# A gated linear-attention recurrence with a mixture of experts on one core: which chunks have their triangular blocks inverted together

## The chip, the cores and the metric

The kernel runs on one core of a Trainium2 chip, as one launch. The metric is the device time of that launch in microseconds (us). The engines are TensorE (PE in the profile; PEld is its weight load), VectorE (DVE), ScalarE (ACT), GpSimd (POOL) and SyncE (SP), which in this kernel only issues DMAs. Each engine runs its instructions in the order in which the program lists them, and waits on semaphores for what the others produce.

## The reference, cut to what matters

For 4 batches and 8 heads there are 768 steps of a 40 x 40 state per head. Each step reads the state, decays it, corrects it by a rank-one term and adds a rank-one term; the attention output then goes through 8 experts:

```python
for t in range(S):                                  # S = 768
    y[:, :, t] = np.einsum('bhd,bhde->bhe', rt, state)
    Sa = np.einsum('bhde,bhe->bhd', state, at)
    state_decay = state * wt[:, :, None, :] - np.einsum('bhd,bhe->bhde', Sa, bt)
    state = state_decay + np.einsum('bhd,bhe->bhde', vt, kt)
...
P = np.exp(x @ w_gate - max)                        # x: 3072 tokens x 320
for _ in range(8):                                  # rows and columns of P normed in turn
    ...
for e in range(E):                                  # E = 8, F = 1024
    out += P[:, e:e + 1] * (np.maximum(x @ w1[e], 0.0) @ w2[e])
```

## The kernel before, in words

**Chunks.** The 768 steps are cut into 12 chunks of 64 steps (c = 0 to 11). Within a chunk the rank-one corrections couple the steps by a strictly triangular 64 x 64 matrix per head, so that a chunk can be done with matmuls once the inverse of the unit triangular matrix is there. Work on a chunk is done per batch, b = 0 to 3, all 8 heads at once. Below, "chunk 9 b0" is batch 0 of chunk 9.

**Preparation** (`prep`, lines 106 to 165), once for each chunk and batch, does not need the state: a load of the inputs (`inp`, line 109), scans on DVE (lines 114 to 124: `q`, a reciprocal, `g`), products on POOL (`cc`, `ab`, `kb`; for the first ones on DVE), matmuls `ll` and transposes `kt` on PE, a mask on DVE (line 155), copies on ACT. The triangular blocks go out of `lt` to DRAM (`ld`, line 148 or 164). Its results are kept in 17 sets of buffers (NSX = 17), used in rotation. So a preparation can run ahead of the recurrence by 17 batches, a little over four chunks, and then waits for a set: preparation number 4c + b writes the set that number 4c + b - 17 has used.

**Inversion.** Line 388 lists groups of chunks that are inverted together. For each group the triangular 32 x 32 diagonal blocks are loaded back from DRAM with one block to a partition: `lu`, line 342, four DMAs for each chunk, which fills 64 partitions. So a pair of chunks takes all 128 partitions. The inversion itself is on DVE alone (lines 167 to 194): per group seven products and seven reductions on the small diagonal blocks (lines 170 and 173), then eight products (line 179) and eight reductions (line 182) on larger ones, then one copy (line 331) that puts the result in another order into the buffer `pr`. These are 31 instructions for any group; the number of chunks in it sets only how many partitions they cover (`us`, line 367). `un`, `lu` and `pr` have one buffer each. After the copy the inverses go to DRAM (`ud` and `nd`, lines 333 and 334) and come back in the layout of the recurrence (`tload`, lines 207 to 217: `lg`, `td`, `tt`). `tmat` (lines 219 to 233) joins the 32 x 32 blocks to 64 x 64 on PE (`gp`, `op`) and ACT.

**Recurrence** (`recur`, lines 235 to 302), for each chunk and batch, depends on the same batch of the chunk before: `av` on PE, the mask `f` on DVE (line 252), `xc` on PE, copies on ACT, `pu` on PE with the inverse `tt` (line 270), the mask `pm` on DVE (line 272), `c2` on PE, `ws` on DVE (line 279), the output `y` and the next state `z` (POOL; `z` on DVE from chunk 9 on), a transpose `zt` and copies into `vz`. The first instruction of a batch that needs the chunk's inverse is `pu`; `pm`, right behind it, is used below as the mark for where a chunk stands. The four batches of a chunk follow each other a few us apart.

**Order.** The events of preparation, inversion and recurrence are sorted by due times (lines 346 to 382). Inside the attention part a scheduler then places the instructions on each engine by its own estimate of their times; it decides which of them lie between the operations of an inversion. The mixture of experts (lines 449 to 734) comes behind: its weights and tokens are split and loaded (`prep_w`, `prep_x`) while the last chunks run, and from its ninth block on its order is written out by hand.

Of the kernel before, what the change touches and what calls it, by code (L numbers as in the profile page):

```python
# [28 lines left out]
def attention(ctx, tc, d, xd, ps, pq, pt, gs, lg):  # L29
# [328 lines left out]
    for c in range(NCH):  # L358
# [5 lines left out]
        for half in range(2):  # L364
            ev.append((t + 2 * SKEW * half, tmat, (c, half)))
    for s, cs in enumerate(GROUPS):
        us = slice(0, 64 * len(cs))
# [17 lines left out]
            pass  # L385


GROUPS = [[0, 1], [2, 3], [4, 5], [6, 7], [8, 9], [10, 11]]
GRP = {c: (i, j) for i, g in enumerate(GROUPS) for j, c in enumerate(g)}
P0 = -8  # L390
PD = 0.75
# [416 lines left out]
```

## Time and profile before

| | before |
|---|---|
| median of 3 runs | 1899.47 us (1899.22 to 1904.73) |
| span of the profiled execution, first to last instruction | 1898.1 us |
| PE busy | 1763.3 us (93%) |
| DVE busy | 1414.6 us (75%) |
| ACT busy | 863.0 us (45%) |
| POOL busy | 939.8 us (50%) |
| first `pm` of chunk 0, of chunk 11 | 125.70 us, 538.93 us from the start |
| start of the copy that ends an inversion (line 331), six of them | 103.43, 166.28, 264.33, 346.15, 428.13, 487.59 us |

The profile gives the profiled execution no time but its span; the median of the runs is 1.4 us above it. Times in the views are us from the start of that span. A row of the timeline has the start, the duration, the engine with its line and operation, and in brackets how long the engine sat idle before it and what ended that. "Busy" counts an instruction's whole duration, and the ends of matmuls are modelled, so that a busy PE need not be at its limit. A name such as `st` or `sx` on DVE's line 155 is one of the 17 sets.

### The profile page before, as it was taken

How to read it: one execution, taken by the hardware profiler on the slowest of the kernel's cores; microseconds unless marked ns; L12 is line 12 of the kernel's file. 1: busy time of each engine (PE TensorE's matmuls, PEld its weight loads, DVE VectorE, ACT ScalarE, POOL GpSimd, SP SyncE). 2: the span in 40 equal slices, each digit the busy share in tenths (PEclk: the TensorE clock that was granted, in tenths of full speed). 3: DMA queues.
4: the chain of work that ended last, by engine and by line, in shares of the span. 5: the costliest groups of instructions: out<-in, count | busy, mean ns of one | idle time of the engine just before them, and what ended most of it. 6: DMA issues, size and time to landing. Idle time of an engine off the chain costs nothing.

```text
span 1898.1 us, 31892 instructions
## 1 busy us (share of the span) xinstructions
PE 1763.3 (93%) x12035; PEld 1723.4 (91%) x12035; DVE 1414.6 (75%) x2330; ACT 863.0 (45%) x1861; POOL 939.8 (50%) x881
## 2 busy tenths in 40 slices
PE   4378989889898999999999999989999999999999
PEld 4368888788888999999999999989999999999999
DVE  7767778687588877676877768996776768777676
ACT  5336565655563444343343434444343433434342
POOL 5636355562254346282643718353562826437170
PEclk9569788989899999999999999999999999999999
DMA  8477776865631111020111102220110201111011
GB/s 189 95 131 149 149 148 136 162 133 123 158 112 62 37 37 55 19 73 19 55 37 37 57 17 73 77 82 34 40 55 19 73 19 55 37 37 55 19 37 42
DMA packets 188414, 139.67 MB, mean 74 GB/s; under 512 B 156005, under 2 KB 165349, under 8 KB 188261
## 3 DMA queue, kind: packets, MB, share of 16 engines
q1 hardware_dynamic: 185061, 132.39, 28.0%
q10 hardware_dynamic: 3200, 5.25, 1.1%
q8 instruction: 95, 1.56, 0.3%
q14 instruction: 58, 0.48, 0.1%
HBM read 117.15 MB, written 20.45 MB: 72 GB/s over the span
## 4 chain that ended last, share of the span: by engine, by line
PE 70%; DVE 10%; DMA 3%; issue 3%; POOL 1%; ACT 1%; SPq 0%; DVEq 0%; POOLq 0%; ACTq 0%
PE op L609 33%; PE p L544 31%; DVE hl L568 1%; PE xc L259 1%; DMA inp<-in_inp_dram 1%; DVE sm L562 1%; DVE pr L179 1%; PE pu L270 1%; PE av L251 1%; PE lp L307 1%; DVE xch L532 1%; PE ll L145 1%; DVE u L562 1%; DMA nd<-pr 1%; PE c L277 1%
## 5 line engine op out<-in xcount | busy, mean ns | idle before, releaser
L544 PE MATMUL p<-xch,wh 128*128 128x384 f32 (+1 forms) x1792 | 606.0, 340 | 13.1 <-DVE u L562 7.5
L565 ACT ACTIVATE hh<-sm 128x384 fp32r<-128x384 f32 x512 | 269.4, 526 | 730.0 <-DVE sm L562 730.0
L609 PE MATMUL op<-wh,hh 128*128 128x320 f32 x1536 | 477.1, 311 | 1.0 <-ACT hh L565 0.9
L609 PE MATMUL op<-wl,hh 128*128 128x320 f32 x1536 | 474.9, 310 | 0.0
L609 PE MATMUL op<-wh,hl 128*128 128x320 f32 x1536 | 468.1, 310 | 5.2 <-DVE hl L568 5.2
L490 POOL TENSOR_TENSOR wl<-ws,wh 128x640 fp32r<-128x640 f32 x64 | 110.7, 1730 | 573.0 <-ACT wh L488 572.8
L568 DVE SCALAR_TENSOR_TENSOR hl<-sm,hh 128x384 fp32r<-128x384 f32 x512 | 375.8, 767 | 2.8 <-ACT hh L565 2.3
L544 PEld LDWEIGHTS p<-xch,wh 128*128 128x128 f32 (+1 forms) x1792 | 337.6, 189 | 18.9 <-DVE u L562 10.3
L544 PE MATMUL p<-xcl,wh 128*128 128x384 f32 x896 | 302.8, 338 | 0.0
L544 PE MATMUL p<-xch,wl 128*128 128x384 f32 x896 | 302.4, 337 | 0.0
L609 PEld LDWEIGHTS op<-wh,hl 128*128 128x128 f32 x1536 | 287.0, 188 | 6.3 <-DVE hl L568 6.1
L609 PEld LDWEIGHTS op<-wh,hh 128*128 128x128 f32 x1536 | 290.5, 189 | 1.6 <-ACT hh L565 1.5
L609 PEld LDWEIGHTS op<-wl,hh 128*128 128x128 f32 x1536 | 291.2, 190 | 0.0
L562 DVE TENSOR_TENSOR sm<-p,u 128x384 f32<-128x384 f32 x384 | 236.4, 625 | 8.8
L544 PEld LDWEIGHTS p<-xcl,wh 128*128 128x128 f32 x896 | 168.8, 188 | 0.0
L544 PEld LDWEIGHTS p<-xch,wl 128*128 128x128 f32 x896 | 168.7, 188 | 0.0
L562 DVE TENSOR_TENSOR sm<-p,p 128x384 f32<-128x384 f32 x128 | 71.3, 557 | 127.8 <-PE p L544 72.6
L562 DVE TENSOR_TENSOR p<-p,p 128x384 f32<-128x384 f32 x128 | 71.1, 556 | 98.9 <-PE p L544 97.3
L562 DVE TENSOR_TENSOR u<-p,p 128x384 f32<-128x384 f32 x128 | 70.8, 553 | 56.6 <-PE p L544 55.4
L145 PE MATMUL ll<-ab,kb 104*128 104x128 f32 x336 | 61.7, 342 | 55.1 <-POOL ab L140 24.2
L498 POOL TENSOR_TENSOR wl<-ss,wh 128x512 fp32r<-128x512 f32 x64 | 96.8, 1513 | 32.1 <-ACT wh L495 27.6
L145 PEld LDWEIGHTS ll<-ab,kb 104*128 104x128 f32 x336 | 53.5, 242 | 59.3 <-POOL ab L140 30.1
(161 smaller groups left out, 2884.1 us busy)
## 6 DMA issues: line engine op xcount, KB each, us to landing
ws<-in_wts_dram SPq DMA_DIRECT2D x64, 832.0 KB
inp<-in_inp_dram SPq DMA_DIRECT2D x42, 521.6 KB
rb<-in_r_dram SPq DMA_DIRECT2D x48, 208.0 KB
ld<-lt ACTq DMA_DIRECT2D x40, 128.0 KB
vz<-in_v_dram SPq DMA_DIRECT2D x48, 104.0 KB
f<-in_vt_dram SPq DMA_DIRECT2D x48, 80.0 KB
xd<-y SPq DMA_DIRECT2D x96, 40.0 KB
st<-in_inp_dram SPq DMA_DIRECT2D x6, 521.6 KB
```

What stands on the lines that cost most here:

```text
L145: nc.tensor.matmul(ll[:, p], lhsT=kb[:, p], rhs=ab[:, p], start=True, stop=True)
L179: nc.vector.tensor_tensor(out=prv, in0=a.unsqueeze(2).broadcast_to([nu, n_c, n_r, n_k]), in1=m.rearrange("u k r -> u r k").unsqueeze(1).br ...
L251: nc.tensor.matmul(av[:, p], lhsT=vz[:, p], rhs=rb[:, p], start=True, stop=True)
L259: nc.tensor.matmul(xc[h][:, p], lhsT=pp["sx"][:, p, h], rhs=f[:, p, h], start=True, stop=True)
L270: nc.tensor.matmul(pu[:, p], lhsT=tts[c][:, b * NP + p], rhs=x1[:, p], start=True, stop=True)
L490: g.tensor_tensor(out=wl[:, 0:640], in0=raw[:, 256:896], in1=wh[:, 0:640], op=ALU.subtract)
L498: g.tensor_tensor(out=lv[:, 3:7], in0=so[:, :, 0], in1=hv[:, 3:7, 0], op=ALU.subtract)
L544: nc.tensor.matmul(o, lhsT=w_, rhs=x_, start=(j == 0), stop=(j == 3))
L562: eng.tensor_tensor(out=out, in0=x, in1=y, op=ALU.add)
L565: nc.scalar.activation(out=hh[:, f, h], in_=sm[f][:, h], func=AF.Relu)
L568: v.scalar_tensor_tensor(out=hl[:, f, h], in0=sm[f][:, h], scalar=0.0, in1=hh[:, f, h], op0=ALU.max, op1=ALU.subtract)
L609: nc.tensor.matmul(ops[i], lhsT=a[:, h, cs], rhs=w_[:, cw], start=(f == 0 and h == 0 and j == 0), stop=(last and h == 1 and j == 2))
```

## The change

Seven groups take the place of six. Chunk 0 is inverted alone, then come the pairs (1, 2), (3, 4), (5, 6), (7, 8) and (9, 10), and chunk 11 is inverted alone:

```diff
-GROUPS = [[0, 1], [2, 3], [4, 5], [6, 7], [8, 9], [10, 11]]
+GROUPS = [[0], [1, 2], [3, 4], [5, 6], [7, 8], [9, 10], [11]]
 GRP = {c: (i, j) for i, g in enumerate(GROUPS) for j, c in enumerate(g)}
```

The due times of the groups follow from the list (line 368: five units to a chunk, less ten), and so does the number of inversions. Nothing else is edited, but the scheduler's order comes out different on every engine.

On SP, at the start of the program, the loads of the first group's triangular blocks (line 342) stood so before, behind the last stores of `ld`:

```order
L148 DMA ld<-st_188 64x512
L342 DMA lu<-ld 16x32x32 x3
L148 DMA ld<-st_187 64x512
L342 DMA lu<-ld 16x32x32
L208 DMA lg<-ld 32x16x32 x2
L164 DMA ld<-lt 64x512 x2
L109 DMA inp<-in_inp_dram 104x1284
L342 DMA lu<-ld 16x32x32 x4
```

and stand so now:

```order
L148 DMA ld<-st_188 64x512
L342 DMA lu<-ld 16x32x32 x4
L148 DMA ld<-st_187 64x512
L208 DMA lg<-ld 32x16x32 x2
L164 DMA ld<-lt 64x512 x2
```

The first group needs four loads where it needed eight, and the second four, behind two stores of chunk 1's blocks and an input, are no longer in front of its first instruction.

On DVE, at the place where chunk 1's first `pm` (line 272) stood before, the second inversion, of chunks 2 and 3, was near its end (`sx_157` is the set of chunk 4 b3):

```order
L182 TENSOR_REDUCE un<-pr 128x16x8
L279 TENSOR_TENSOR ws<-c_1257,c_203 104x416
L114 SCALAR_TENSOR_TENSOR q<-inp,cst 104x260
L272 TENSOR_TENSOR pm<-pu,cst 128x416
L179 TENSOR_TENSOR pr<-gt,un 128x2048
L118 RECIPROCAL g_196<-q 104x4
L155 TENSOR_TENSOR sx_157<-ll,cst 64x8x64
L182 TENSOR_REDUCE un<-pr 128x16x8
```

The same `pm` now (the `L272` in the last row) stands behind the first operations of the third inversion, of chunks 3 and 4 (`sx_161` is the set of chunk 5 b0):

```order
L155 TENSOR_TENSOR sx_161<-ll,cst 64x8x64
L170 TENSOR_TENSOR pr<-un,lu 128x4
L312 COPY lg<-lp 64x8
L173 TENSOR_REDUCE un<-pr 128x4
L170 TENSOR_TENSOR pr<-un,lu 128x16
L173 TENSOR_REDUCE un<-pr 128x4x2
L170 TENSOR_TENSOR pr<-un,lu 128x36
L173 TENSOR_REDUCE un<-pr 128x4x3
L170 TENSOR_TENSOR pr<-un,lu 128x64
L114 SCALAR_TENSOR_TENSOR q<-inp,cst 104x260
L173 TENSOR_REDUCE un<-pr 128x4x4
L272 TENSOR_TENSOR pm<-pu,cst 128x416
```

The second inversion, which chunk 1 now belongs to, has ended ahead of these rows.

On DVE in chunk 9, from its first `pm` to its first `ws` (line 279), there were two operations of the sixth inversion's last part before:

```order
L272 TENSOR_TENSOR pm<-pu,cst 128x416
L182 TENSOR_REDUCE gt<-pr 128x128
L252 TENSOR_TENSOR f<-av,cst 104x8x64
L179 TENSOR_TENSOR pr<-gt,un 128x1024
L279 TENSOR_TENSOR ws<-c_4745,c_202 104x416
```

and there are these of the new seventh, of chunk 11 alone, now:

```order
L272 TENSOR_TENSOR pm<-pu,cst 128x416
L179 TENSOR_TENSOR pr<-un,lu 64x512
L182 TENSOR_REDUCE gt<-pr 64x64
L179 TENSOR_TENSOR pr<-gt,un 64x512
L182 TENSOR_REDUCE un<-pr 64x8x8
L179 TENSOR_TENSOR pr<-un,lu 64x2048
L312 COPY lg<-lp 64x8
L252 TENSOR_TENSOR f<-av,cst 104x8x64
L182 TENSOR_REDUCE gt<-pr 64x128
L179 TENSOR_TENSOR pr<-un,lu 64x1024
L279 TENSOR_TENSOR ws<-c_4779,c_202 104x416
```

Eight operations of an inversion stand between the two where two stood. The copy that ends the seventh inversion follows chunk 9's third `pm`, as the copy of the sixth did before.

## The prediction

> **What bounds the kernel now.** I read the windows by stage first, then the chain of waits, then the timeline of one instruction per chunk. Columns of the windows are stretch, length, busy time of PE, PEld, DVE, ACT and POOL, granted clock, DMA share, GB/s.
>
> ```profile
> 104.50:560.00 455.50, 405.71 (x3622) 378.53 (x3623) 327.07 (x507) 273.12 (x678) 219.39 (x240) 0.87 0.68 143
> 650.00:1898.00 1248.00, 1234.47 (x7727) 1230.75 (x7725) 928.59 (x1554) 508.26 (x1000) 615.12 (x527) 1.00 0.13 45
> ...
> 293.00:347.20 54.20, 48.09 (x455) 44.43 (x453) 50.14 (x77) 35.27 (x89) 37.42 (x35) 0.97 0.65 139
> 347.20:371.70 24.50, 22.49 (x223) 21.25 (x223) 11.56 (x21) 17.13 (x44) 14.29 (x20) 0.93 0.82 172
> ```
>
> The experts (second row) are PE's, 99% busy, and the change leaves them alone: they move as a block with the end of the attention part. There two kinds of stretches alternate: while an inversion runs (the third row, the fourth inversion) DVE is 93% busy, and in the pause before the next 47%. The chain of waits (start, length, what) passes from one to the other so:
>
> ```profile
> 429.18 4.08 DMA nd<-pr
> 433.68 2.06 DMA td<-nd
> ```
>
> The result of an inversion goes through DRAM and then to PE. Here are the copies that end two inversions (L331), the start of one (L170), and the first `pm` (L272) of chunks 3, 4, 6, 8, 9, 10 and 11:
>
> ```profile
> 241.55 0.59 DVE L272 TENSOR_TENSOR pm<-pu,cst 128x416 f32<-128x416 f32 x1 [0.59 <-PE pu L270]
> 264.33 1.02 DVE L331 COPY pr<-un 128x1024 f32<-128x1024 f32 x1
> 281.73 0.56 DVE L272 TENSOR_TENSOR pm<-pu,cst 128x416 f32<-128x416 f32 x1
> 362.07 0.56 DVE L272 TENSOR_TENSOR pm<-pu,cst 128x416 f32<-128x416 f32 x1
> 371.72 0.17 DVE L170 TENSOR_TENSOR pr<-un,lu 128x4 f32<-128x4 f32 x1 [2.78 <-DMA lu<-ld]
> 428.13 1.02 DVE L331 COPY pr<-un 128x1024 f32<-128x1024 f32 x1
> 442.09 0.59 DVE L272 TENSOR_TENSOR pm<-pu,cst 128x416 f32<-128x416 f32 x1 [1.00 <-PE pu L270]
> 473.02 0.58 DVE L272 TENSOR_TENSOR pm<-pu,cst 128x416 f32<-128x416 f32 x1
> 504.68 0.59 DVE L272 TENSOR_TENSOR pm<-pu,cst 128x416 f32<-128x416 f32 x1 [1.81 <-PE pu L270]
> 538.93 0.57 DVE L272 TENSOR_TENSOR pm<-pu,cst 128x416 f32<-128x416 f32 x1
> ```
>
> A pair's first `pm` follows the copy by 17.4 and 14.0 us. So the attention part is a loop: recurrence frees sets, preparation fills them, inversion, recurrence. Two chunks take 80.3 and 80.0 us (281.73 to 362.07 to 442.09), and chunks 8 to 10, with no preparation beside them, 62.6 us. The place of chunk 11's first `pm`, 538.93, measures the whole part; 1898.1 - 538.93 = 1359.2 us follow.
>
> **The change part by part.** I build that one time anew, from the head.
>
> *An inversion costs the same for one chunk as for two.* The groups of the first 700 us:
>
> ```profile
> L179 DVE TENSOR_TENSOR pr<-gt,un 128x512 f32<-128x512 f32 (+2 forms) x24 | 46.9, 1953 | 0.1
> L179 DVE TENSOR_TENSOR pr<-un,lu 128x512 f32<-128x512 f32 (+2 forms) x24 | 46.5, 1938 | 0.1
> L182 DVE TENSOR_REDUCE gt<-pr 128x64 f32<-128x512 f32 (+2 forms) x24 | 29.0, 1209 | 0.1
> L182 DVE TENSOR_REDUCE un<-pr 128x64 f32<-128x512 f32 (+2 forms) x24 | 28.9, 1205 | 0.1
> L170 DVE TENSOR_TENSOR pr<-un,lu 128x4 f32<-128x4 f32 (+6 forms) x42 | 15.2, 362 | 10.5 <-DMA lu<-ld 6.1 <-DMA tt<-ud 3.5
> L173 DVE TENSOR_REDUCE un<-pr 128x4 f32<-128x4 f32 (+6 forms) x42 | 9.8, 234 | 1.0
> L252 DVE TENSOR_TENSOR f<-av,cst 104x512 f32<-104x512 f32 x48 | 32.7, 681 | 18.6 <-PE av L251 17.8 <-DMA td<-ud 0.6
> L155 DVE TENSOR_TENSOR sx<-ll,cst 64x512 f32<-64x512 f32 x27 | 18.1, 671 | 10.5 <-PE ll L145 10.4
> ```
>
> The sum of the six inversion groups is 176.3 us, 29.4 for one, with its copy (1.0) 30.4. The last two rows decide what 64 partitions cost: two masks with 512 elements to a partition take 681 and 671 ns on 104 and 64 partitions. So a seventh inversion adds 30.4 us of DVE. The number of blocks loaded, prepared and multiplied is unchanged.
>
> *The first inversion starts earlier.*
>
> ```profile
> 40.47 1.46 SPq L342 DMA_DIRECT2D lu<-ld  x3
> 53.20 1.90 SPq L342 DMA_DIRECT2D lu<-ld  x4
> 60.37 0.17 DVE L170 TENSOR_TENSOR pr<-un,lu 128x4 f32<-128x4 f32 x1 [1.76 <-DMA lu<-ld]
> 103.43 1.00 DVE L331 COPY pr<-un 128x1024 f32<-128x1024 f32 x1
> ```
>
> It waits for its eighth load, issued until 55.1 and landed 5.3 us later. Chunk 0's four go out from 40.47 in a row, until 42.4, and should have landed by 48: 12.4 us earlier. With the same 43 us its copy starts at 91. The bounds of this gain: 0 (if other transfers in the queues hold these loads up as long) and 18.0 (60.37 - 42.4, a landing at once); I take the delay that the eight loads showed.
>
> *The second, chunks 1 and 2, follows at once.* Its `pr` must be out (the DMA of `nd` ended 5.1 us after the start of the copy, 429.18 + 4.08 - 428.13), so it starts at 96. Its window holds fewer rows of the recurrence than that of 371.72 to 428.13 (56.4 us); against the 53.7 us of the window of 210.65 to 264.33 (below), I take 49. The copy starts at 145.
>
> *Then a wait.* In the changed order chunk 1's first `pm` stands on DVE behind nine operations of the third inversion, of chunks 3 and 4, which needs chunk 4 b3 prepared. Its mask comes about 7 us after the start of that copy: the copy itself, 1.0, and between them the scans of one preparation and four rows of 0.6 to 0.7 us, with a wait of PE for the last `c2`; I take 152. From such a mask to the inversion's first operation:
>
> ```profile
> 194.11 0.67 DVE L155 TENSOR_TENSOR sx<-ll,cst 64x512 f32<-64x512 f32 x1
> 195.01 0.59 ACT L159 ACTIVATE lt<-ll 64x512 f32<-64x512 f32 x1 [0.69 <-DMA ld<-lt]
> 203.18 1.90 SPq L342 DMA_DIRECT2D lu<-ld  x4
> 210.65 0.17 DVE L170 TENSOR_TENSOR pr<-un,lu 128x4 f32<-128x4 f32 x1 [1.55 <-DMA lu<-ld]
> ```
>
> 16.5 us by the store and the loads; it could be 9.0 if the loads went out right behind ACT's copy (0.9 + 0.6 + 7.5). The store and its landing are in every one, so I take the 16.5. So the third inversion starts at 168, with 53.7 us its copy starts at 222, and chunk 3's first `pm` follows 17 to 20 us later at 239 to 242. I take 241; before it was 241.55. **The head start is used up there**: an inversion that stood in the idle time of the head now stands beside chunk 0, and chunk 1 waits for its own. Late behind chunk 1's `pm` are its `c2`, `ws` and state, and so all of chunk 2.
>
> *The middle keeps its period.* The same rows lie between two ends of inversions, so chunk 7 comes two periods (160.4 us) on, at 401.
>
> *The tail.* The inversion of chunks 9 and 10 starts 9.7 us after that (362.07 to 371.72) and lasts 56.4 us less four preparations' scans and two masks: the changed order has two preparations' scans in that window, where the one of 371.72 to 428.13 has six (groups between 371.5 and 429.5):
>
> ```profile
> L114 DVE TENSOR_TENSOR_SCAN q<-inp,cst 104x260 f32<-104x260 f32 x6 | 4.3, 710 | 5.3 <-DMA inp<-in_inp_dram 5.3
> L122 DVE TENSOR_TENSOR_SCAN st<-inp,g 104x256 f32<-104x256 f32 x4 | 3.9, 984 | 0.1
> ```
>
> 4 x 1.7 + 2 x 0.67 = 8 us: 48. Its copy is at 459, chunk 9's first `pm` 15 us later at 474. Before, chunk 10 stood 31.7 us behind it. Now the rest of the seventh inversion is in between on DVE: of its 30.4 us the small operations (25.0 / 6 = 4.2), four operations of 512 elements and the copy are elsewhere,
>
> ```profile
> 459.13 1.05 DVE L179 TENSOR_TENSOR pr<-un,lu 128x512 f32<-128x512 f32 x1
> 460.70 0.67 DVE L182 TENSOR_REDUCE gt<-pr 128x64 f32<-128x512 f32 x1
> 527.88 0.68 DVE L252 TENSOR_TENSOR f<-av,cst 104x512 f32<-104x512 f32 x1
> ```
>
> which leaves 30.4 - 4.2 - 3.4 - 1.0 = 21.8, and with some 5 us of masks and sums 27 us until chunk 10's first `f`. From chunk 11's `f` (527.88) to its `pm` (538.93) are 11 us. So chunk 10 comes 38 us behind chunk 9, at 512; the bounds are 31.7 (all covered) and 31.7 + 21.8 = 53.5 (nothing covered). Chunk 11 follows after 34.2 us (504.68 to 538.93), at 546. That is 7 us later than before, and nothing behind it regains them, since PE is busy all the time.
>
> [...] On POOL a copy of 4 elements to a partition took 3.55 us beside one of DVE's long products:
>
> ```profile
> 78.48 3.64 DVE L179 TENSOR_TENSOR pr<-un,lu 128x2048 f32<-128x2048 f32 x1
> 78.62 3.55 POOL L138 COPY st<-q 104x4 f32<-104x4 f32 x1 [0.80 <-DVE q L114]
> 106.16 0.19 POOL L138 COPY st<-q 104x4 f32<-104x4 f32 x1
> ```
>
> Alone it took 0.19. [...]
>
> **Sum:** 1898.1 + 7 = 1905 us for the profiled execution, and with the 1.4 us by which the median lies above it **1907 us**, 0.4% slower.
>
> **The rivals.** *PE is the bound.* In the attention part it is 89% busy (405.71 of 455.5), in the pause of DVE 92% (22.49 of 24.5), and the work on it is the same. Then the 12.4 us of the head remain, the extra inversion lies in DVE's idle time (455.5 - 327 = 128 us), and the time is 1899.5 - 12 = 1887. Against it: a pair's `pm` still waits out the way of `nd` and `td` after each inversion.
>
> *No change.* If the third inversion waits only the 9.0 us of the lower bound, and chunk 1 with it, 7 us of the head start are kept, and the tail's 7 take them: 1900 us. For it speaks that chunk 1 could go on at 163 (145 and the 17.4); against it, that DVE's order puts it behind the load.
>
> *The seventh inversion is exposed whole.* If the way from chunk 9's first `pm` to chunk 10's is lengthened by all 21.8 us, as it is when each batch waits on DVE for a long product in turn, the 15.5 us from 38 to 53.5 come on top of my 7: 1922. It decides if chunk 10's first `f` comes later than 27 us behind chunk 9's `pm`. Against it: the windows above show PE at work beside inversions.
>
> *The change does nothing:* excluded, the order shows seven inversions, two of them on 64 partitions.
>
> **How the numbers follow.** My forecast 0.44, PE as the bound 0.24, no change 0.2, the whole exposure 0.12. Of the forecast's own range, 1901 to 1912 (the head start 12 +-1, the window of the second inversion 47 to 51, the tail's 38 +-3), about a third is within 0.3%, which is 5.7 us and about what a measurement of this kernel can tell from no change: 0.14 of its 0.44. Of the rival "no change" 0.15 is within it, 0.04 slower and 0.01 faster. So: slower 0.30 + 0.04 + 0.12 = 0.46, same 0.14 + 0.15 = 0.29, faster 0.24 + 0.01 = 0.25. The range goes from 1888, a little above the first rival, to 1920, a little below the third.
>
> **What would show it.** In the changed profile the first copy of line 331 should stand near 91, the second near 145, the third near 222, the fourth to sixth 80 us apart; chunk 1's first `pm` at 170 or later and behind a wait for `lu`; chunk 3's near 241, chunk 9's near 474, chunk 10's 38 us behind it. I am wrong if chunk 3 comes before 235 (the head start survives), if the period in the middle is not 80 us, or if chunk 10 follows within 33 us.

## The result, and the profile after

The changed kernel took 1933.16 us (median of 4 runs, 1922.66 to 1941.5) against 1901.91 us for the kernel before: a ratio of 1.0156, 95% interval 1.0115 to 1.0197. The profiled execution of the changed kernel took 1931.21 us, its span is 1929.1 us, 31 us more than the 1898.1 of before. The forecast was 1907 us in a range of 1888 to 1920. The sign was right, the size was more than four times too small.

The windows by stage of the changed kernel (columns as in the prediction: stretch, length, busy time of PE, PEld, DVE, ACT, POOL, granted clock, DMA share, GB/s). The first row is the attention part, the second the experts, the third the fourth inversion and the fourth the pause behind it:

```profile
88.00:590.00 502.00, 453.77 (x3663) 420.64 (x3664) 367.79 (x551) 278.47 (x691) 237.17 (x248) 0.80 0.62 133
680.00:1928.00 1248.00, 1234.77 (x7725) 1231.06 (x7724) 926.06 (x1554) 508.54 (x1000) 614.21 (x527) 1.00 0.14 45
255.10:307.80 52.70, 46.61 (x396) 43.49 (x395) 48.89 (x73) 32.33 (x82) 30.42 (x29) 0.87 0.66 136
307.80:332.40 24.60, 23.00 (x206) 21.91 (x204) 11.81 (x21) 15.36 (x40) 11.95 (x18) 0.79 0.80 167
```

The experts are the block they were. In the attention part, from the end of the first copy to some 22 us behind chunk 11's first `pm` in each kernel, PE shows 48 us more of busy time for nearly the same matmuls, and the granted clock is 0.80 where it was 0.87. (The profile counts two matmuls for each one of the program: four calls of `pu` are its `pu` x8. Counts in views are the profile's.) That column stood in the first rows that the prediction quoted, and no step of it used it.

The timeline of the changed kernel: the copies that end the first three inversions and the sixth, the start of the third and of the seventh, the first `pm` of chunks 1, 3, 7, 9, 10 and 11, and the third `pm` of chunk 9 (507.36):

```profile
86.71 1.02 DVE L331 COPY pr<-un 64x1024 f32<-64x1024 f32 x1
139.24 1.98 DVE L331 COPY pr<-un 128x1024 f32<-128x1024 f32 x1
157.66 0.17 DVE L170 TENSOR_TENSOR pr<-un,lu 128x4 f32<-128x4 f32 x1 [1.26 <-DMA lu<-ld]
161.66 0.58 DVE L272 TENSOR_TENSOR pm<-pu,cst 128x416 f32<-128x416 f32 x1
208.52 1.29 DVE L331 COPY pr<-un 128x1024 f32<-128x1024 f32 x1
242.68 0.59 DVE L272 TENSOR_TENSOR pm<-pu,cst 128x416 f32<-128x416 f32 x1 [0.71 <-PE pu L270]
405.27 0.59 DVE L272 TENSOR_TENSOR pm<-pu,cst 128x416 f32<-128x416 f32 x1 [1.03 <-PE pu L270]
465.80 1.04 DVE L331 COPY pr<-un 128x1024 f32<-128x1024 f32 x1
471.90 0.15 DVE L170 TENSOR_TENSOR pr<-un,lu 64x4 f32<-64x4 f32 x1 [0.52 <-DMA nd<-pr]
480.62 0.57 DVE L272 TENSOR_TENSOR pm<-pu,cst 128x416 f32<-128x416 f32 x1
507.36 0.57 DVE L272 TENSOR_TENSOR pm<-pu,cst 128x416 f32<-128x416 f32 x1
531.27 0.59 DVE L272 TENSOR_TENSOR pm<-pu,cst 128x416 f32<-128x416 f32 x1 [1.27 <-PE pu L270]
567.27 0.58 DVE L272 TENSOR_TENSOR pm<-pu,cst 128x416 f32<-128x416 f32 x1
```

Up to chunk 7 nothing is lost: its first `pm` is at 405.27, as in the kernel before. Chunk 9 is 7.6 us late (480.62 against 473.02). Then chunk 10 comes 50.7 us behind chunk 9, where it was 31.7. Chunk 11 is 28.3 us late, and that is nearly all of the result. The windows of 10 us in that stretch, of the changed kernel:

```profile
480.00:490.00 10.00, 10.00 (x58) 8.79 (x57) 9.84 (x10) 3.01 (x8) 0.00 (x0) 0.50 0.47 94
490.00:500.00 10.00, 10.00 (x58) 9.10 (x57) 9.04 (x10) 3.50 (x9) 0.86 (x1) 0.50 0.31 52
510.00:520.00 10.00, 10.00 (x64) 9.60 (x63) 2.69 (x5) 4.50 (x12) 0.87 (x1) 0.50 0.40 94
520.00:530.00 10.00, 10.00 (x55) 8.81 (x53) 2.35 (x5) 2.65 (x7) 0.27 (x1) 0.50 0.50 105
530.00:540.00 10.00, 10.00 (x79) 9.47 (x78) 2.71 (x6) 4.93 (x13) 4.07 (x6) 0.72 0.67 219
```

and of the kernel before:

```profile
480.00:490.00 10.00, 7.57 (x73) 6.85 (x72) 9.66 (x10) 5.52 (x14) 0.73 (x1) 1.00 0.39 90
490.00:500.00 10.00, 7.74 (x81) 7.46 (x79) 3.03 (x6) 4.98 (x14) 0.87 (x1) 0.84 0.73 160
500.00:510.00 10.00, 9.66 (x77) 9.32 (x77) 1.60 (x4) 3.41 (x8) 0.72 (x1) 0.64 0.83 207
```

From 480 to 530 us PE runs at half clock. It is shown as busy all the time, and does 55 to 64 matmuls in 10 us. From chunk 9's first `pm` to chunk 10's it has no gap at all: 50.65 us of work, 285 matmuls. In the kernel before it was busy for 26.6 of 31.7 us there, with 253 matmuls at a mean clock of 0.88. The last reduction of the seventh inversion ends at 507; from 510 on DVE is idle three quarters of the time, and the pace doesn't recover. The chain of waits of the changed kernel says the same (start, length, what):

```profile
478.20 2.03 PE pu L270 x8
480.24 0.69 PE xc L259 x4
...
487.01 1.84 PE gp L226 x16
488.85 0.81 PE zt L297 x4
489.66 1.39 PE c L277 x8
491.05 1.71 PE pu L270 x8
```

It is PE alone, one group of matmuls behind the other, where the chain of before passed to DVE and DMA (its row for the wait of chunk 10's inverse is the first below). At a granted clock of 1.00 `pu` takes half as long, 1.06 us for 2.04, as two rows of it in the changed kernel show, at half clock and behind the end of the stretch (second below).

```profile
492.85 2.59 DMA td<-nd
```

```profile
504.69 2.04 PE L270 MATMUL pu<-x,tt 128*128 128x104 f32 x8
...
537.65 1.06 PE L270 MATMUL pu<-x,tt 128*128 128x104 f32 x8
```

Where does DVE wait? In the groups of the first 700 us of the changed kernel, the mask `f` now idles 32.4 us for PE's `av`, where it idled 17.8. A DVE that held up PE would idle less:

```profile
L252 DVE TENSOR_TENSOR f<-av,cst 104x512 f32<-104x512 f32 x48 | 32.7, 681 | 32.4 <-PE av L251 32.4
```

### The profile page after: what moved, and what is told of

The parts are those of the page before. It is cut to its first block, busy times and chain, and to the rows that moved or that the text cites. A ratio compares the mean times of both kernels' runs of the same rounds, so it can differ in the third digit from the quotient of the medians.

```text
span 1929.1 us, 31920 instructions
## 1 busy us (share of the span) xinstructions
PE 1804.4 (94%) x12035; PEld 1758.9 (91%) x12035; DVE 1446.1 (75%) x2361; ACT 864.4 (45%) x1861; POOL 943.5 (49%) x881
## 3 DMA queue, kind: packets, MB, share of 16 engines
q8 instruction: 95, 1.56, 0.3%
## 4 chain that ended last, share of the span: by engine, by line
PE 70%; DVE 9%; DMA 3%; issue 2%; POOL 1%; ACT 1%; SPq 0%; DVEq 0%; POOLq 0%; ACTq 0%
PE op L609 32%; PE p L544 30%; PE xc L259 2%; PE pu L270 1%; DVE hl L568 1%; DVE sm L562 1%; PE av L251 1%; DMA inp<-in_inp_dram 1%; PE c L277 1%; PE lp L307 1%; PE gp L226 1%; DVE pr L179 1%; DVE u L562 1%; PE op L231 1%; DVE xch L527 1%
```

## The experiments

**The theories.** A: what is lost is the clock. The inversions change the order, PE is filled less densely, its granted clock falls to half, and PE's own work doubles. B: the seventh inversion's operations lengthen chunk 9 on DVE (the prediction's rival of the whole exposure). C: a seventh inversion costs its 30 us of DVE wherever it stands. These are theories; what the runs bear out of them follows. "Lost clock" below is the span times (1 - mean granted clock) of a run.

**Another place for the extra inversion.** Three lists of groups:

```diff
+GROUPS = [[0], [1], [2, 3], [4, 5], [6, 7], [8, 9], [10, 11]]     # head_only
+GROUPS = [[0], [1, 2], [3, 4], [5, 6], [7, 8], [9], [10, 11]]     # lone9
+GROUPS = [[0, 1], [2, 3], [4, 5], [6, 7], [8, 9], [10], [11]]     # tail_only
```

> Groups [0], [1], [2, 3] to [10, 11]: seven inversions, the extra one in the head, the tail as before. Theory A (the extra inversion costs where it stands beside chunk 9, with no preparation left to keep PE going, and PE's granted clock falls to 0.5 there): the tail is as before, chunk 9 to 10 in 31 to 35 us, chunk 10 to 11 in 34, chunk 11's first pm at 530 to 541, time 1890 to 1903 us. Theory B (the operations of the seventh inversion lengthen chunk 9 on DVE, whatever the clock): the same here. Theory C (any seventh inversion costs its 30 us of DVE wherever it stands): chunk 11 at 565 to 570, 1925 to 1933 us.

> Groups [0], [1, 2], [3, 4], [5, 6], [7, 8], [9], [10, 11]: the head of the change, its extra inversion moved from chunk 11 to chunk 9, the last pair as before. Theories A and B: chunk 7 at 405 as in the change; the inversion of chunk 9 stands beside chunk 7 where preparations still run; chunk 9 at 475 to 490, chunk 9 to 11 in 66 to 72 us, time 1900 to 1915 us. Theory C: chunk 11 at 565 to 570, 1925 to 1933 us.

> Groups [0, 1] to [8, 9], then [10], [11]: the head as before, two lone inversions at the end. Theories A and B: up to chunk 8 as before (442), then 20 to 30 us late at chunk 11 (559 to 570), time 1918 to 1932 us; A sees the granted clock at 0.5 to 0.6 for 40 us or more beside chunk 9 or 10, B no lower clock than before (0.8 to 1). If the change's loss came from its head instead, the time is 1900 us here.

Measured: head_only 1925.91 us (ratio 1.0140, 1.0094 to 1.0186), lone9 1925.68 (1.0139, 1.0095 to 1.0183), tail_only 1921.65 (1.0113, 1.0080 to 1.0145). So the place decides little, against A and B as I had put them (only tail_only fell into their range); the time is nearly the one of C. Yet the lost microseconds are in other places in each: in the profiled executions, chunk 9 to 10 takes 29.0 us in head_only, 34.3 in lone9 and 29.5 in tail_only, and the longer half-clock stretches from 430 us on stand at 510 to 544 in head_only, at 440 to 461, 519 to 529 and 567 to 594 in lone9, and at 431 to 469 and 503 to 520 in tail_only.

**The seventh inversion without its products.**

```diff
-        for i, (fn, a) in enumerate(INV):
+        for i, (fn, a) in enumerate(INV[:7] if cs == [11] else INV):
```

> The changed kernel without the eight large products and eight reductions (lines 179 and 182) of the last group [11]: its small products, its copy, its stores and loads stay; the off-diagonal part of chunk 11's inverse is then not computed. Theories A and B: chunk 9 at 480 as in the change, chunk 9 to 10 back to 31 to 36 us and chunk 10 to 11 to 34, chunk 11 at 546 to 551, time 1908 to 1914 us; A also expects the granted clock from 480 to 530 back at 0.8 or more. Rival D (the loads, the stores and their landing delay chunk 9, not the products): chunk 9 to 10 stays at 45 us or more, time 1925 us or more.

Measured: 1927.49 us (1.0143, 1.0091 to 1.0194). The windows of this kernel:

```profile
480.00:490.00 10.00, 10.00 (x57) 8.79 (x56) 1.44 (x3) 2.81 (x7) 0.00 (x0) 0.50 0.76 178
490.00:500.00 10.00, 10.00 (x88) 9.15 (x87) 1.51 (x3) 4.42 (x12) 3.62 (x5) 0.88 1.01 226
500.00:510.00 10.00, 7.66 (x48) 7.01 (x48) 4.33 (x11) 2.76 (x7) 0.87 (x1) 0.63 0.65 142
```

DVE is nearly idle beside chunk 9, and the time stays. That speaks against B and C as costs of DVE's time: 16 of the 31 operations, 25 of the inversion's 30 us (the four large groups in the prediction, by six), are left out, and the loss is the same within the intervals, which leave room for some 12 us either way. The clock is still down here, for 13.7 us from 479 on and four more times until 571. Chunk 9 to 10 took 40.3 us, 10 less than in the change, but chunk 10 to 11 took 41.0; A and B expected 31 to 36 and 34, and A a clock of 0.8 or more, so A failed as put too. Of rival D the time came true (1925 us or more), but not its 45 us or more for chunk 9 to 10.

**PE kept at work.** Matmuls repeated into a tile that nothing reads, in the changed kernel and in the one before:

```diff
+    def warm(c, w, x, k=2):                      # k=4 in warm4
+        if c not in (9, 10):
+            return
+        dm = pq.tile([128, NP, 128], F32, name="dm", tag="pq")
+        for _ in range(k):
+            for p in range(NP):
+                nc.tensor.matmul(dm[...], lhsT=w[:, p], rhs=x[:, p], start=True, stop=True)
...
+        warm(c, vz, rb)                          # behind av; so too behind pu and c2
```

> The changed kernel with 24 more matmuls for each batch of chunks 9 and 10: av, pu and c2 are each repeated twice, right behind the originals and with the same inputs, into a PSUM tile that nothing reads. DVE's order is that of the change. 96 matmuls a chunk at 0.11 us (pu x8 0.90 us) are 11 us more of PE for each of the two chunks at full clock. Theory A (PE's granted clock is what is lost beside chunk 9): the extra work keeps the clock up, 0.8 or more from 480 to 530 where it was 0.5; chunk 9 to 10 takes 34 to 42 us instead of 50.7, in spite of more work; time 1908 to 1920 us. Rival (the clock is low only because the work waits, and costs nothing): chunk 9 to 10 takes 50 to 62 us, time 1930 to 1950 us.

> As the run with two repeats, with four: 192 more matmuls a chunk, 22 us at full clock. Theory A: clock 0.9 or more from 480 to 530, chunk 9 to 10 in 38 to 46 us, since now the added work itself begins to count; time 1910 to 1925 us. Rival: chunk 9 to 10 in 62 to 75 us, time 1950 us or more.

> The kernel before with the same repeats in chunks 9 and 10. There the clock stood at 0.92, 0.82, 0.83 from 480 to 540, and at 0.64 from 500 to 510. Theory A: little to win, 1893 to 1908 us; chunk 9 to 10 in 30 to 36 us. Rival: the added 22 us of PE work show at least in half, 1911 us or more.

Measured: warm2 1943.0 us (1.0194), warm4 1985.62 (1.0392), warm2_before 1933.44 (1.0143). All three expectations of A on the time failed, and all three times lie in the rival's ranges. A window of warm2, and then one of warm2_before:

```profile
500.00:520.00 20.00, 20.00 (x190) 18.84 (x190) 14.13 (x14) 6.84 (x17) 1.69 (x2) 1.00 0.48 126
```

```profile
480.00:500.00 20.00, 20.00 (x190) 18.84 (x190) 4.11 (x10) 7.65 (x20) 4.67 (x6) 1.00 0.84 223
```

The clock did come up to 1.00, but now PE is full, with 190 matmuls in 20 us, and each added one counts. My price for them was half of what they take: I counted the program's 96 matmuls a chunk at the 0.11 us of one of the profile's, but the trace shows two for each, 384 in warm2, so that two chunks get some 40 us of added work (an estimate from 0.11 us each), not 22. The pair is useful all the same: at a mean clock of 0.97 in both, chunk 9 to chunk 11 takes 97.7 us with the seventh inversion beside it and 98.0 with the six of before (486.6 to 584.3, and 468.1 to 566.1). And by the ratios the same matmuls cost some 27 us in the kernel before, but 7 in the changed one. Lost clock went from 133 to 105 us in the changed one and from 106 to 95 in the one before. The scheduler's order on DVE came out different in both, though, so not all of this need be the matmuls'.

**One burst, and a thin repeat.** In kick9 c2's matmuls are repeated eight times, for b0 and b2 of chunk 9 alone; in warm_av only av is repeated, once, in chunks 9 and 10:

```diff
+        if (c, b) in ((9, 0), (9, 2)):
+            warm(c, pp["bb"], pm)                # kick9, k=8
...
+        warm(c, vz, rb)                          # warm_av, k=1, c in (9, 10)
```

> The changed kernel with two bursts of 32 matmuls in chunk 9, behind the c2 of b0 and of b2 (c2's own matmuls repeated eight times into a tile that nothing reads), and nothing else. In the change the granted clock fell to 0.5 at 478 us and stayed there for 57 us without a break. A burst is 6.7 us of unbroken work at half clock, 3.4 at full, so the two add 7 to 13 us of PE work. Theory A: the first burst brings the clock back, so that the half-clock stretch of 57 us falls to 25 us or less, and some 15 to 20 us of lost clock return against 7 to 10 us of added work: chunk 9 to 10 in 40 to 46 us, 1918 to 1928 us. Rival (added work only adds): 1938 to 1946 us, chunk 9 to 10 at 56 us or more.

> The changed kernel with av repeated once for each batch of chunks 9 and 10: 32 short matmuls in all, 3.4 us at full clock, none of them a burst. Theory A: too thin to hold the clock for certain; 1922 to 1935 us, going with the mean clock of each run. Rival: 1936 us and more.

> The kernel before with av repeated once for each batch of chunks 9 and 10 (32 matmuls, 3.4 us at full clock). In the change the same 32 matmuls brought the ratio from 1.0156 to 1.0090. Clock theory: before has little half-clock time to win there (10 and 5 us in two dips, against 58 us in the change), so no such gain: 1898 to 1908 us. If the repeats help by another way than the clock: 1890 us or less.

Measured for kick9: 1932.62 us (1.0142, 1.0111 to 1.0174), so no gain, and a time in neither range. Chunk 9 to 10 took 47.6 us, also in neither. Its windows have the clock up in chunk 9 all the same:

```profile
480.00:490.00 10.00, 10.00 (x57) 8.79 (x57) 9.86 (x10) 3.29 (x8) 0.00 (x0) 0.50 0.46 94
490.00:500.00 10.00, 10.00 (x103) 9.65 (x101) 9.89 (x8) 1.37 (x4) 0.87 (x1) 0.94 0.30 50
510.00:520.00 10.00, 10.00 (x115) 9.68 (x114) 1.61 (x3) 4.05 (x11) 3.46 (x5) 1.00 0.92 286
```

The first window is nearly that of the changed kernel. The half-clock stretch is 13.6 us long instead of 58: the clock is back at 491.1, only 0.6 us behind the first matmul of the burst (490.54). In cut7 the clock came back after 13.7 us with no burst at all. So it is not shown that the burst raised the clock; over the six runs kick9 lost 115 us of clock, the changed kernel over its four 133.

In kick9's timeline (`pm` is on line 279 here) stand the last long product of the seventh inversion, the second and the third `pm` of chunk 9 and the first of chunk 10:

```profile
497.70 3.74 DVE L179 TENSOR_TENSOR pr<-gt,un 64x2048 f32<-64x2048 f32 x1
503.68 0.57 DVE L279 TENSOR_TENSOR pm<-pu,cst 128x416 f32<-128x416 f32 x1
507.92 0.59 DVE L279 TENSOR_TENSOR pm<-pu,cst 128x416 f32<-128x416 f32 x1 [0.66 <-PE pu L277]
...
527.81 0.59 DVE L279 TENSOR_TENSOR pm<-pu,cst 128x416 f32<-128x416 f32 x1 [0.23 <-PE pu L277]
```

Here the second `pm` stands behind the last products and reductions of the seventh inversion, which in the changed kernel come behind it, so the ways from that `pm` on can't be compared. From the third `pm` on they can: of the inversion the changed kernel has only the copy left there, and kick9 nothing. To chunk 10's first `pm` it is 19.9 us in kick9 at a clock of 0.99, the second burst included, and 23.9 in the changed kernel (507.36 to 531.27) at 0.50. PE is busy without a gap in both, with 202 matmuls (64 of them the burst's) against 139. Without the burst's some 6 us, an estimate worked out below, kick9 would take some 14. So that half of the stretch is as long as PE's work is at half clock. The first half, with the inversion's work beside it, has no such pair. Why no gain then? A burst is 64 of the profile's matmuls, some 6 us at full clock (52 of them took 4.85 us, and the third window above has 115 in 10 us at 1.00), twice what I had put. From the first `pm` to the second takes 23.5 us instead of 14.3, with the burst and four more operations of the inversion in between. And the clock fell again at 542 and 552 us, for 6.8 and 13.7 us: chunk 10 to 11 took 40.8 us.

warm_av took 1923.7 us (1.0090, 1.0061 to 1.0119): with the program's 32 matmuls more the change is 0.66% faster than without; the two intervals overlap a little (the change's begins at 1.0115). The same 32 matmuls made the kernel before slower, 1908.0 us (1.0035, 1.0010 to 1.0059). That is what A expects. But warm_av's order on DVE beside chunk 9 differs from the change's too, and the next experiment shows that an order alone moves the time as much.

**Other orders, with six and with seven groups.** One due time is shifted, in both kernels:

```diff
-P0 = -8            +P0 = -7.5          # p0_later, after_p0
-T_LEAD = 2         +T_LEAD = 1.5       # before_tlead, after_tlead
-L_LEAD = 0.5       +L_LEAD = 1         # before_llead, after_llead
-INV_DT = 0.05      +INV_DT = 0.3       # before_invdt, after_invdt
```

> The kernel before with its six pairs, and only the due time of the preparations half a unit later (P0 = -7.5 instead of -8): the scheduler's order differs in 640 lines on DVE, and no inversion is added. The four runs before this showed 21 to 27 us more for each of four kernels with a seventh inversion, wherever it stood and even with most of its products left out. If the seventh inversion is the cause (theories B, C): 1895 to 1905 us here. If what is lost is the clock, and depends on how densely the order fills PE (A), another order may lose too: 1900 to 1925 us, with the loss in the stretches where the granted clock is lower than before.

> The change with the preparations due half a unit later (P0 = -7.5), seven inversions in another order (814 lines of difference on DVE). The same step made the kernel before 0.75% slower with no inversion added. If an order's fill of PE sets the lost clock, and the order before was the favourable one (A): anywhere between 1905 and 1940 us, on the line on which all runs so far lie, span = 1807 + 0.92 x span x (1 - mean clock), within 9 us. If the seventh inversion costs its 25 to 30 us whatever the order (C): 1925 to 1945 us.

> The kernel before, six pairs, with the inverses joined half a unit later (T_LEAD = 1.5 instead of 2): a third order without an added inversion (588 lines of difference on DVE). A: 1895 to 1925 us, on the same line. If only a seventh inversion costs (C): 1895 to 1905 us.

> The change with T_LEAD = 1.5; the six pairs with this step were 0.64% slower than before (1918 us). Order alone: 1905 to 1935 us; a cost of the seventh inversion's own: 1926 to 1938 us.

> Six pairs, the loads of the inverses half a unit earlier (L_LEAD = 1 instead of 0.5): a fourth order without an added inversion. If before's order is a favourable one among many (order theory): 1908 to 1925 us, on the line of span against lost clock. If only a seventh inversion costs (C): 1895 to 1905 us.

> The change with the same L_LEAD = 1. If the order alone decides: 1905 to 1935 us, in the same band as the six-pair orders (1908 to 1925). If the seventh inversion adds a cost of its own on top: about as far above the six-pair kernel with this step as the change is above the other shifted six-pair orders, 8 to 20 us, so 1920 to 1940 us.

> Six pairs, the operations of an inversion due 0.3 units apart instead of 0.05: a small change of order (63 lines of difference on DVE). Order theory: between 1898 and 1920 us, going with the mean granted clock. C: 1895 to 1905 us.

> The change with the same spacing of 0.3. Order alone: 1905 to 1935 us; a cost of the seventh inversion's own: 8 to 20 us above the six-pair kernel with this step.

Ratios to the kernel before with their intervals, and beside them mean span and mean lost clock of the runs in us:

| shift | six groups | span, lost | seven groups | span, lost |
|---|---|---|---|---|
| none | 1 | 1901, 106 | 1.0156 (1.0115 to 1.0197) | 1930, 133 |
| P0 | 1.0075 (1.0043 to 1.0107) | 1917, 122 | 1.0135 (1.0097 to 1.0174) | 1929, 129 |
| T_LEAD | 1.0064 (1.0035 to 1.0093) | 1916, 114 | 1.0102 (1.0078 to 1.0125) | 1919, 121 |
| L_LEAD | 1.0044 (1.0009 to 1.0079) | 1910, 113 | 1.0125 (1.0087 to 1.0163) | 1925, 134 |
| INV_DT | 0.9996 (0.9975 to 1.0017) | 1900, 104 | 1.0146 (1.0091 to 1.0202) | 1929, 130 |

Of these eight expectations the ranges of A and of the order alone all held. That only a seventh inversion costs failed in three of the four orders with six groups, and a cost of its own of 1926 us or more failed in after_tlead (1921 us). By its ratio every order with seven groups is slower than every order with six (the nearest two, T_LEAD with seven and P0 with six, have intervals that overlap). The means are 1.0036 and 1.0133. So of the change's 30 us, as a rough estimate from five pairs that differ by 0.38 to 1.56%, some 18 us (0.97% of 1902) go with seven groups in whatever order; some 7 us are a favourable order that the kernel before had, since three of the four shifts that add nothing also lose; and the last 5 are an order a little worse than the mean of seven. So a cost of seven groups is there, as in C, but cut7 speaks against DVE's time as its cause.

Span and lost clock go together. Over 146 runs of these ten kernels and the three with another place for the inversion, a straight line with a step gives span = 1824 + 0.74 x lost + 7.5 if there are seven groups. The 17 us of clock that seven groups lose on average (126 against 108) then carry 13 us, and 7.5 us remain at equal clock. A line alone doesn't say which of the two is the cause. For chunk 9 the traces do; for the rest of the attention part it stays argued.

after_tlead speaks against B a second time. It has the long operations of the seventh inversion beside chunk 9 (all of 1024 and 2048 elements, and the copy), and the clock happened to be up. Its windows, and its timeline with the first `pm` of chunks 9 and 10 and the two longest products of the seventh inversion between:

```profile
490.00:500.00 10.00, 10.00 (x92) 9.17 (x90) 9.88 (x12) 4.41 (x12) 1.96 (x2) 0.90 0.67 129
500.00:510.00 10.00, 10.00 (x110) 9.36 (x110) 9.94 (x13) 5.25 (x14) 3.07 (x2) 1.00 0.55 105
510.00:520.00 10.00, 8.99 (x90) 8.16 (x89) 9.94 (x11) 5.98 (x15) 1.05 (x2) 0.97 0.31 67
```

```profile
493.89 0.58 DVE L272 TENSOR_TENSOR pm<-pu,cst 128x416 f32<-128x416 f32 x1
495.09 3.76 DVE L179 TENSOR_TENSOR pr<-un,lu 64x2048 f32<-64x2048 f32 x1
...
512.02 3.75 DVE L179 TENSOR_TENSOR pr<-gt,un 64x2048 f32<-64x2048 f32 x1
...
523.13 0.59 DVE L272 TENSOR_TENSOR pm<-pu,cst 128x416 f32<-128x416 f32 x1 [0.46 <-PE pu L270]
```

DVE is 99% busy, and chunk 10 follows in 29.2 us, faster than in the kernel before (31.7). PE does 274 matmuls there in 28.2 us of busy time at a mean clock of 0.94, where the changed kernel took 50.65 us for 285 at 0.50. This kernel had lost its time ahead of that, with 27.3 us at half clock from 440 on. So with the clock up, and in this order, the seventh inversion's operations don't make chunk 9 longer than it was before. The order of DVE's operations within the chunk differs from the change's. after_invdt has exactly that of the change there, from the first `pm` of chunk 9 to that of chunk 10, and in it the clock was down for 58.0 us once more (from 481 on) and the chunk took 50.6 us; so what the change's own order would take at full clock no run shows.

None of the eighteen kernels beats the kernel before; before_invdt equals it.

## Why the prediction was wrong, by its own steps

**An inversion costs the same for one chunk as for two: right.** In kick9's and after_tlead's rows a product of 64x2048 takes 3.74 to 3.76 us, beside the 3.64 of 128x2048 in the prediction. Over the span DVE is busy for 31.5 us more (1414.6 to 1446.1), forecast 30.4.

**The first inversion starts earlier, the second follows: right, and a little better.** Copies at 86.7 and 139.2 us, forecast 91 and 145.

**"Then a wait", to 241: right in its sum by luck, wrong in its parts.** The mask that the third inversion needs came at 147.4 (forecast 152), and the inversion began 10.2 us behind it, near the lower bound of 9.0 and not at the 16.5 that I took. So chunk 1's first `pm` came at 161.7, not "at 170 or later", and behind eight operations of that inversion, not nine, as the rows ahead of the prediction show. The third copy came at 208.5 instead of 222. But chunk 3's first `pm` followed 34 us later, not 17 to 20, at 242.7: chunk 2 stood between, and PE was busy for 31.8 of these 34.2 us at a mean clock of 0.76. Chunk 2 to chunk 3 took 45.9 us, where it took 41.8 before. So the head start was used up as forecast, but not by the wait for the loads.

**The middle keeps its period: right.** Chunk 3 to 7 took 162.6 us, forecast 160.4; 405.3 against 401. The sixth inversion then took 48.7 us, forecast 48, and chunk 9 stood 14.8 us behind its copy, forecast 15.

**The tail: the step that failed.** I put chunk 9 at 474 (measured 480.6) and chunk 10 38 us behind it, and said that the answer between 31.7 and 53.5 hangs on how much of the seventh inversion's 21.8 us on DVE is covered. It was 50.7, within these bounds but not by that mechanism. In its place stands PE's half clock: PE worked at a clock of 0.50 without a gap from one `pm` to the other. Without the inversion's long operations the kernel is no faster (cut7, though chunk 9 to 10 is 10 us shorter there), and with them chunk 10 follows in 29.2 us when the clock is up (after_tlead). The sum took PE's durations as given and had no term for the clock, though 0.87 stood in the first row it quoted. Its part on DVE was not bad: the 27 us to chunk 10's first `f` were 26.5 in after_tlead, but 44.7 in the change, where PE delivered late. And the 11 us from `f` to `pm`, which it read at chunk 11, were 2.8 in after_tlead; where it read them, 6.8 us at half clock begin at 531.0. Chunk 11's step of 34.2 us was 36.0, and some 3 us more were lost behind it. (Between chunk 9's first `pm` and first `ws` the rows of the change show seven operations of the inversion, not eight; the sum didn't use that number.)

**The rivals.** "The seventh inversion is exposed whole" came nearest, with 53.5 us for 50.7 and 1922 for 1933, and its condition came true: chunk 10's first `f` was late. Yet its mechanism is not what the trace shows, since PE never waited for DVE in that stretch: had only the times of the profile after been read, they would have seemed to confirm it. "PE is the bound" was nearer to the mechanism than its 1887 shows: at half clock PE is the bound of chunk 9. "No change" had the head right up to chunk 1 (10.2 us against its 9.0, and 161.7 against its 163), but the head start did not last until chunk 3.

**What a measurement can tell.** I put 0.3%. Single runs of the kernel before ranged from 1891.75 to 1918.56 us, 1.4%. Over 73 of them, span follows lost clock with 0.65 us per us (correlation 0.89). A difference below 1% therefore rests on the mean of several runs of each kernel.

**What stays open:** what in an order makes the clock fall. Seven groups lose more clock than six with the same shift in every pair tried, also where the extra inversion stands in the head, and I can't say from an order where or for how long the clock will be down. That PE is filled less densely (theory A) is not shown: PE was busy without a gap where the clock stayed down longest.

## What to carry to other kernels

Where PE shows busy at a granted clock under 1, price the clock: lost clock is span times (1 - clock), it was 106 us of 1901 here, and the orders tried lost between 104 and 122 us with six groups and between 121 and 134 with seven. A change of order is best judged against several orders of both kernels, since a shift that adds nothing moved the time by as much as 0.75%. And when a loss stands beside the suspected work, take the work away before believing it.

## What the runs showed of the hardware that was not expected

**The stretches of low clock last a multiple of 3.4 us.** From 140 to 620 us, in windows of 1 us, the clock of both kernels reads 0.50 or 1.00 but for the edges of a stretch. Two rows at the start and two at the end of the long stretch of the changed kernel:

```profile
477.00:478.00 1.00, 1.00 (x15) 0.96 (x13) 0.97 (x1) 0.57 (x2) 0.00 (x0) 0.80 0.49 102
478.00:479.00 1.00, 0.92 (x6) 0.83 (x5) 0.86 (x4) 0.15 (x1) 0.72 (x1) 0.50 0.78 268
...
535.00:536.00 1.00, 1.00 (x8) 0.86 (x6) 0.00 (x0) 0.65 (x2) 0.00 (x0) 0.69 0.01 2
536.00:537.00 1.00, 1.00 (x14) 0.96 (x14) 0.69 (x1) 0.34 (x1) 0.00 (x0) 1.00 0.49 82
```

Twice the share missing from 1, summed over a stretch, gives its length. From 140 us on the kernel before has lengths of 3.4, 6.8, 10.3, 13.7 and 17.1 us, 95.5 us in all up to 620; the changed kernel has 177.2, with one of 58.0, which is 17 times 3.41. What makes the clock fall or come back at a given time, no run here shows, nor why one program's runs differ in it (the four of the changed kernel have a mean clock of 0.923 to 0.938).

**The profile shows PE busy all the time, and the clock did not come back.** In the changed kernel PE was busy for 55.00 us from 480 to 535, and the clock stayed at 0.50; the whole stretch is 58 us. In kick9 and in cut7 the clock came back after 13.6 and 13.7 us; what brought it back, no run here tells.
